# Another order of the same 1418 steps, with 41 changes of ScalarE's table in place of 43

## The chip, the cores and the metric

The kernel runs on one core of one Trainium2 chip. The metric is the device time of one execution in microseconds (us). TensorE (PE) multiplies matrices, VectorE (DVE), ScalarE (ACT) and GpSimd (POOL) work on elements, SyncE (SP) issues most transfers (DMA). Each engine takes its own instructions strictly in order; between engines, semaphores make a step wait for what it reads.

## The reference

A gated linear attention with a complex decay is followed by a gated feed-forward block with a residual. Inputs are q, k, v, a_re and a_im of shape (4, 8, 768, 48): 4 batches, 8 heads, 768 tokens, 48 dimensions a head.

```
a = (a_re, a_im) * min(mag, 0.999) / (mag + 1e-6)          mag = |a_re + i a_im|
for t in range(768):
    S = a[t] * S + k[t] v[t]^T          (complex S of 48 x 48 for each batch and head)
    y[t] = q[t] . Re S
x = y as (3072, 384)
g, val = x @ w_gate, x @ w_val          (384 -> 1536)
out = x + sigmoid(x @ w_res) * ((gelu(g) * val) @ w_out)
```

## The kernel before

The 768 tokens are cut into 6 chunks of 128. A tile is one chunk of one batch, 24 in all. Tiles are taken in 14 units: units 0 and 1 have one tile of chunk 0 each, unit 2 has two, units 3 to 10 have two each (two units to a chunk), unit 11 has two tiles of chunk 5, and units 12 and 13 one each. The body writes out the steps of each unit in three functions.

- `prepare` loads ar, ai, q, k, v (L420), takes ln and exp of a_re (L442, L443), multiplies t by a_im (L445), squares (L448 on ACT or L450), takes another ln (L451) and joins them to the log of the decay (L452, L456). Sums over the tokens of a chunk are matmuls with a triangular mask (L402, or L406 in float32 for units 0 to 2). exp of the sums gives E and Ei (L487, L488); the angle goes through an arctangent (L497), the same kind of sum, a rounding (L524 or L527, L529), an absolute value (L536 or L538) and two sines (L542). q times E and k times Ei (L548) times the sines give the features fQ and fK (L553). Units 0 to 5 transpose the features on PE (L569) and copy them (L377 or L378); units 6 to 13 use DMA transposes issued by SP (L562), four for a unit of two tiles. A row of E and one of the angle are carried to the next chunk by small DMAs that POOL issues (L492, L503, L509).
- `attend` multiplies features (scores, L610), masks them (L615), multiplies with v and the carried state (L626, L628), copies the result x (L377 or L378) and updates the state (L642, L665 to L685).
- `forward` transposes x (L708 on PE, or by DMA), runs the gate and value matmuls (L726), gelu (L736), the product (L737), the residual gate (L748, L751) and the output matmuls (L761), then L765, L768 and the store (L770). A forward of a one-tile unit uses 128 columns a matmul, of a two-tile unit 256.

PE also has 30 warm-up steps of four matmuls (L777). POOL issues the weights' DMAs (L384): w_gate and w_val in two halves of three pieces each, then w_res and w_out.

ACT holds one set of functions at a time: "L" has ln and exp, "T" arctangent and sine, "G" gelu and tanh; squares, copies and roundings run with any. Whenever a step needs another set than the last one, the program puts in a table load (L785 in the trace).

The order of everything is a literal list. `ORDER` has the numbers of all 1418 steps; each engine gets its steps in that order. `PLACE` says on which engine a step runs that could run on several; a step that is not in it takes a default. The core of the loop:

```
for j in order:
    t = self.steps[j]
    for x in t.stores:                       # a buffer is bound when it is first used:
        ...
        x.index = min(range(x.bufs), key=lambda i: row[i])   # the one that came free first in the list
        ...
    if t.act is not None and t.act != table:
        table = t.act
        load(table)
    ins = t.fn()
    if t.port:                               # POOL's steps and some of DVE's: each change of
        if last is not None and last[0] != t.eng:            # engine waits for the step before
            turn(ins, last[1])
        last = (t.eng, ins)
```

So the list also decides which load waits for which buffer (24 of [128, 768] are shared by loads and temporaries), and where DVE and POOL hand over.

Of the kernel before, what the change touches and what calls it, by code (L numbers as in the profile page):

```python
# [47 lines left out]
    53: "POOL", 54: "DVE", 67: "DVE", 77: "DVE", 80: "ACT", 119: "POOL", 120: "POOL", 131: "DVE", 136: "POOL", 137: "POOL",  # L48
    152: "DVE", 155: "ACT", 190: "DVE", 191: "DVE", 210: "DVE", 218: "ACT", 220: "DVE", 224: "DVE", 239: "DVE", 303: "POOL",
    319: "POOL", 324: "DVE", 326: "DVE", 330: "POOL", 336: "DVE", 349: "DVE", 355: "DVE", 359: "DVE", 406: "DVE", 425: "POOL",  # L50
    433: "ACT", 436: "POOL", 439: "DVE", 441: "DVE", 443: "DVE", 447: "POOL", 455: "ACT", 457: "DVE", 458: "ACT", 475: "DVE",
    476: "ACT", 482: "ACT", 523: "DVE", 538: "POOL", 542: "POOL", 550: "ACT", 553: "POOL", 558: "DVE", 560: "DVE", 564: "POOL",
    570: "DVE", 574: "DVE", 593: "ACT", 655: "POOL", 670: "POOL", 673: "DVE", 677: "DVE", 681: "POOL", 690: "ACT", 696: "DVE",
    706: "DVE", 709: "DVE", 710: "DVE", 780: "ACT", 783: "POOL", 788: "DVE", 790: "DVE", 794: "POOL", 803: "ACT", 809: "DVE",
    815: "DVE", 818: "DVE", 825: "ACT", 881: "POOL", 885: "POOL", 899: "DVE", 901: "DVE", 903: "DVE", 906: "POOL", 907: "POOL",
    914: "ACT", 922: "DVE", 931: "DVE", 932: "ACT", 940: "ACT", 979: "DVE", 1006: "ACT", 1009: "POOL", 1016: "DVE",
    1019: "POOL", 1020: "POOL", 1029: "ACT", 1035: "DVE", 1041: "DVE", 1044: "POOL", 1047: "POOL", 1084: "DVE", 1104: "DVE",
    1105: "POOL", 1120: "POOL", 1130: "POOL", 1131: "POOL", 1138: "ACT", 1140: "ACT", 1146: "DVE", 1152: "DVE", 1155: "POOL",
    1213: "DVE", 1227: "POOL", 1232: "DVE", 1234: "DVE", 1237: "POOL", 1238: "POOL", 1245: "DVE", 1312: "POOL", 1318: "POOL",
    1322: "DVE", 1325: "POOL", 1326: "POOL", 1331: "DVE", 1337: "DVE", 1367: "POOL", 1371: "POOL", 1379: "DVE", 1381: "DVE",  # L60
    1390: "ACT", 1396: "DVE", 1416: "DVE",
}
ORDER = [
# [754 lines left out]
```

## Time and profile before

| | |
|---|---|
| median of 3 runs | 241.28 us (240.02 to 242.72) |
| the profiled execution | 243.0 us, span 241.1 us |
| granted TensorE clock | 1.0 throughout |
| ACT table loads | 43, 55.2 us in all |
| HBM read, written | 31.26 MB, 4.72 MB |
| DMA share by queue | 76.1% SP's, 10.3% POOL's |

The span runs from the first to the last instruction of the profile. A row of a timeline has the start, the length, the engine, the source line, the operation, output <- inputs, shapes and the number of instructions that were merged; in brackets stands how long the engine had been idle before it and what ended that.

### The profile page before, as it was taken

To read this page: it belongs to the slowest core of one execution; us is meant where nothing else is said; L and a number is where in the kernel's file an instruction comes from. 1 tells how busy PE (TensorE), PEld (TensorE's weight loads), DVE (VectorE), ACT (ScalarE), POOL (GpSimd) and SP (SyncE) were. 2 spreads that over 40 slices of the span, in tenths; PEclk is the share of its full clock that TensorE was granted. 3 is DMA by queue.
4 is the path that set the end of the run, shared out by engine and by line. 5 is a ranking of instruction groups with operands and counts; after the bars stand their busy time and mean duration, and the time that the engine had idled before them with its cause. 6 is when DMAs were issued, how large, how long until landed. Compare 5 with 4: busy or idle time off the path is not lost. (4 is left out here: it accounts for less than half of the span.)

```text
span 241.1 us, 6430 instructions
## 1 busy us (share of the span) xinstructions
PE 227.3 (94%) x2513; PEld 180.3 (75%) x2513; DVE 203.5 (84%) x361; ACT 203.8 (85%) x326; POOL 135.5 (56%) x152
## 2 busy tenths in 40 slices
PE   6899997999999999999997999998999999998992
PEld 4677896877788778778785777786788687787871
DVE  2477996999998999999998899998999979976162
ACT  5799996999999999999999899999889889942140
POOL 3457975526987446854929727719759564040111
PEclk9999999999999999999999999999999999999999
DMA  7999999999899989999899999899688283680121
GB/s 146 215 212 219 205 197 183 190 202 187 162 214 217 204 172 202 207 211 200 179 202 184 223 195 180 187 218 193 127 120 191 56 154 85 135 123 16 52 98 67
DMA packets 164798, 40.55 MB, mean 168 GB/s; under 512 B 158240, under 2 KB 164768, under 8 KB 164768
## 3 DMA queue, kind: packets, MB, share of 16 engines
q1 hardware_dynamic: 160320, 36.25, 76.1%
q0 software_dynamic: 4448, 3.90, 10.3%
q8 instruction: 19, 0.31, 0.6%
q14 instruction: 11, 0.09, 0.1%
HBM read 31.26 MB, written 4.72 MB: 149 GB/s over the span
## 5 line engine op out<-in xcount | busy, mean ns | idle before, releaser
L726 PE MATMUL pb<-xT,wv 128*128 128x256 bf16 (+1 forms) x504 | 57.0, 257 | 1.7 <-DMA wv<-in_moe_w_val_dram 1.5
L785 ACT ACT_TABLE_LOAD x43 | 55.2, 1283 | 1.5 <-PEq L802 0.7
L761 PE MATMUL pb<-wo,hb 128*128 128x384 bf16 x288 | 54.6, 326 | 0.0
L726 PE MATMUL pb<-xT,wg 128*128 128x256 bf16 (+1 forms) x504 | 53.5, 257 | 0.0
L737 DVE SCALAR_TENSOR_TENSOR hb<-hb,pb 128x512 bf16<-128x512 bf16 x72 | 47.0, 679 | 7.6 <-PE pb L726 7.4
L736 ACT ACTIVATE hb<-pb 128x512 bf16<-128x512 f32 x72 | 39.5, 608 | 14.2 <-PE pb L726 13.8
L726 PEld LDWEIGHTS <-wv 128*128 128x128 bf16 x504 | 42.8, 98 | 8.5 <-DMA wv<-in_moe_w_val_dram 2.2
L726 PEld LDWEIGHTS <-wg 128*128 128x128 bf16 x504 | 42.8, 98 | 5.6 <-DVE xT L378 0.2
L761 PEld LDWEIGHTS <-hb 128*128 128x128 bf16 x288 | 26.3, 97 | 13.7
L615 DVE TENSOR_TENSOR am<-pb,mask 128x512 bf16<-128x512 f32 x48 | 31.2, 683 | 2.8 <-PE pb L610 2.7
L768 POOL TENSOR_TENSOR ot<-ot,x 128x384 f32<-128x384 f32 x19 | 17.2, 909 | 21.1 <-DVE ot L765 17.0
L548 POOL TENSOR_TENSOR Ke<-k,Ei 128x768 bf16<-128x768 f32 (+1 forms) x11 | 18.3, 1662 | 4.9 <-ACT Ei L488 2.2
L445 POOL TENSOR_TENSOR t<-t,ai 128x768 f32<-128x768 f32 (+1 forms) x11 | 16.7, 1516 | 7.2 <-DMA ai<-in_a_im_dram 3.3
L610 PE MATMUL pb<-QT,KT 96*128 96x128 bf16 x192 | 17.2, 219 | 3.7 <-DMA KT<-fK 2.2
L610 PEld LDWEIGHTS <-KT 96*128 96x128 bf16 x192 | 13.1, 97 | 8.3 <-DMA KT<-fK 3.2
L517 POOL TENSOR_TENSOR tl<-t 128x768 f16<-128x768 f32 (+1 forms) x9 | 12.5, 1391 | 11.6 <-DMA t<-fr 5.1
L777 PE MATMUL pb<-tri,ident 128*128 128x256 bf16 x120 | 16.4, 292 | 2.4 <-POOL tri masks.py:66 2.4
L777 PEld LDWEIGHTS <-ident 128*128 128x128 bf16 x120 | 12.4, 105 | 5.6 <-issue 1.8
L765 DVE SCALAR_TENSOR_TENSOR ot<-sg,pb 128x384 f32<-128x384 f32 x24 | 13.0, 547 | 3.5 <-PE pb L761 2.6
L748 PE MATMUL pb<-wr,xT 128*128 128x384 bf16 x72 | 15.5, 326 | 0.0
L452 DVE SCALAR_TENSOR_TENSOR la<-s,la 128x768 f32<-128x768 f32 (+1 forms) x14 | 11.7, 837 | 3.4 <-POOL s L450 2.1
L529 DVE SCALAR_TENSOR_TENSOR fr<-fr,pb 128x384 f32<-128x384 int32 x24 | 12.8, 546 | 1.5 <-ACT fr L524 1.4
(95 smaller groups left out, 446.8 us busy)
## 6 DMA issues: line engine op xcount, KB each, us to landing
ar<-in_a_re_dram SPq DMA_DIRECT2D x24, 192.0 KB, 3.9
ai<-in_a_im_dram SPq DMA_DIRECT2D x24, 192.0 KB, 3.9
k<-in_k_dram SPq DMA_DIRECT2D x24, 192.0 KB, 4.1
q<-in_q_dram SPq DMA_DIRECT2D x24, 192.0 KB, 3.9
vf<-in_v_dram SPq DMA_DIRECT2D x24, 192.0 KB, 3.8
out_dram<-ot SPq DMA_DIRECT2D x24, 192.0 KB, 3.2
wg<-in_moe_w_gate_dram POOLq DMA_DIRECT2D x6, 192.0 KB, 5.6
wv<-in_moe_w_val_dram POOLq DMA_DIRECT2D x6, 192.0 KB, 6.7
```

What stands on the lines that cost most here:

```text
L445: add(e1, "tai", lambda: on[e1].tensor_tensor(out=F("t"), in0=F("t"), in1=flat(T("ai"), n), op=OP.mult), [s["ai"]], [s["t"]], n)
L548: add(e13, "qe", lambda g=g, src=src, mag=mag, e13=e13: on[e13].tensor_tensor(out=T(g + "e")[:, 0:n * H].rearrange("p x u d -> p (x u d)") ...
L610: nc.tensor.matmul(out=view()[:, h, :], lhsT=kT.tile[0:DD, u * H // 2 + h, :], rhs=qT.tile[0:DD, u * H // 2 + h, :], start=True, stop=True)
L615: add("DVE", "am", lambda u=u, am=am, view=view: nc.vector.tensor_tensor(out=am.tile[:, u * H // 2:(u + 1) * H // 2, :], in0=view(), in1=m ...
L726: nc.tensor.matmul(out=o_.at(y, nb, n * 128)[:, u, :], lhsT=w_[:, k_, (nb * m + u) * 128:(nb * m + u + 1) * 128], rhs=xt.tile[:, k_, 0:n]. ...
L736: add("ACT", "gelu", lambda gp=gp, hv=hv: nc.scalar.activation(out=hv(), in_=pv(gp), func=AF.Gelu), gs, [hh], sz, "G")
L737: add("DVE", "h", lambda vp=vp, hv=hv: nc.vector.scalar_tensor_tensor(out=hv(), in0=hv(), scalar=0.5, in1=pv(vp), op0=OP.mult, op1=OP.mult ...
L748: nc.tensor.matmul(out=rp.at(y, DM), lhsT=xt.tile[:, k_, j, :], rhs=wr[:, k_, :], start=(k_ == 0), stop=(k_ == KF - 1))
L761: nc.tensor.matmul(out=op_.at(0, DM), lhsT=hb[k_ // per].tile[:, (u * n + j) * 128:(u * n + j + 1) * 128], rhs=wo[:, k_, :], start=(k_ == ...
L768: add(e8, "otx", lambda s=s, i=i, ot=ot, e8=e8: on[e8].tensor_tensor(out=ot.tile, in0=ot.tile, in1=s["x"].tile[:, i].rearrange("p h d -> p ...
L777: nc.tensor.matmul(out=spare.at(0, 256), lhsT=ident, rhs=tri[:, :].bitcast(BF), start=True, stop=True)
L785: plan.run(ORDER, lambda table: nc.scalar.preload_act_table_set(ACT_SETS[table]), lambda ins, prev: tc.add_manual_dep(ins.ins, prev.ins.na ...
```

## The change

The code is the same; the literals `PLACE` and `ORDER` are new. No step is added or dropped, and no buffer changes in number or size. The start of each list, and the part where unit 7's features are transposed (797 to 800 are its four DMA transposes: QT and KT of its first tile, then of its second; 804, 806 and 810, 812 are the scores of the first and the second tile):

```
-    14, 46, 51, 52, 24, 22, 20, 8, 19, 1, 112, 117, 118, 23, 47, 53, 54, 55, 113, 3, 49, 119, 28, 120, 180, 9, 63, 129, 130,
+    112, 117, 118, 12, 19, 14, 46, 51, 7, 1, 27, 28, 2, 52, 5, 25, 47, 53, 54, 113, 119, 120, 178, 180, 63, 64, 9, 179, 0, 50,
...
-    902, 797, 800, 716, 718, 799, 720, 897, 899, 736, 798, 593, 705, 801, 722, 1099, 887, 876, 890, 891, 1102, 728, 1211, 993,
+    1095, 895, 721, 518, 723, 735, 715, 736, 716, 800, 725, 883, 799, 896, 704, 797, 733, 717, 898, 897, 737, 594, 801, 884,
+    705, 739, 798, 718, 595, 724, 899, 885, 900, 632, 901, 887, 726, 720, 596, 740, 597, 886, 728, 640, 902, 890, 722, 524,
```

What this makes of each engine's own order, read from the two programs (u is the unit, f the group of a forward):

```
POOL, start, before: tai.u0 tai.u1 sq.u1 mrd.u0 w qe.u1 w w mrd.u1 qe.u1 w w w vcast.u1 mrc.u0 vcast.u0 mrc.u1 tai.u3 wr sq.u3 w mrd.u2 w w w carry.u3 w carry.u3 w
POOL, start, after:  qe.u0 qe.u1 w mrd.u0 mrd.u1 w w w qe.u1 w w mrc.u1 tai.u3 wr mrc.u0 w w w w mrd.u2 w carry.u3 carry.u3 w
ACT, start, before:  [L] ln.u0 exp.u0 ln.u1 exp.u1 lnb.u0 [T] atan.u0 atan.u1 [L] ln.u2 lnb.u1 ...
ACT, start, after:   [L] ln.u1 exp.u1 ln.u0 exp.u0 [T] atan.u0 atan.u1 [L] lnb.u0 lnb.u1 ln.u2 ...
DVE, start, before:  sq.u0 la.u0 cap.u0 round.u1 ...
DVE, start, after:   tai.u0 sq.u0 tai.u1 sq.u1 la.u0 cap.u0 la.u1 fr.u0 cap.u1 tai.u2 ...
ACT, end, before:    gelu.f10 x4 [L] pexpE.u12 x.u11 pexpI.u12 [T] sin.u12 x2 x.u11 [L] pexpI.u13 Mc.u10 pexpE.u13 [T] sin.u13 x2 [G] tanh.f10 ...
ACT, end, after:     gelu.f10 x3 [L] pexpI.u13 pexpE.u13 pexpI.u12 x.u11 pexpE.u12 mrc.u10 [T] sin.u12 x2 round.u13 sin.u13 x2 [G] tanh.f10 ...
```

Here w is a weight's DMA, tai the product with a_im, sq the square, lnb the second ln, la and cap the two steps to the decay's log, pexpE and pexpI the exponentials L487 and L488, qe the products L548, mrd and mrc a carried row and its copy, Mc the copy of the matrix made from it.

Steps that are on another engine than before, as the change in count (a two-tile step has 768 columns, a one-tile step 384):

| step | ACT | DVE | POOL |
|---|---|---|---|
| tai, one tile | | 0 to 3 | 4 to 1 |
| square, one tile; two tiles | 1 to 2; 4 to 6 | 1 to 2; 1 to 1 | 2 to 0; 5 to 3 |
| low part of the decay (L460), one tile; two tiles | | 0 to 2; 6 to 3 | 2 to 0; 3 to 6 |
| low part of the angle (L517), one tile; two tiles | | 1 to 0; 1 to 2 | 1 to 2; 8 to 7 |
| absolute value, one tile; two tiles | 1 to 2; 1 to 2 | 3 to 2; 9 to 8 | |
| q or k product (L548), one tile | | 4 to 3 | 4 to 5 |
| v to bfloat16, one tile; two tiles | 1 to 1; 3 to 4 | 1 to 3; 1 to 0 | 2 to 0; 6 to 6 |
| residual sum (L768) | | 5 to 7 | 19 to 17 |
| copies of x, xT, QT and KT, M | 10 to 11, 3 to 4, 5 to 4, 5 to 8 | 14 to 13, 15 to 14, 15 to 16, 6 to 3 | |
| state (Gb copy; Gb; Gf), carried row's copy | 4 to 2; ; ; 4 to 4 | 3 to 5; 1 to 0; 4 to 3; 0 to 2 | 9 to 9; 3 to 4; 8 to 9; 7 to 5 |

More of the change, by code (lines that the diff above doesn't have):

```diff
@@ L47 @@
 PLACE = {
[L48 to L60, printed above, removed]
@@ L61 @@
-    1390: "ACT", 1396: "DVE", 1416: "DVE",
+    54: "DVE", 71: "POOL", 77: "DVE", 78: "DVE", 80: "ACT", 89: "DVE", 110: "DVE", 120: "DVE", 131: "DVE", 133: "DVE",
+    136: "POOL", 137: "POOL", 143: "DVE", 144: "ACT", 146: "ACT", 152: "DVE", 155: "DVE", 190: "DVE", 191: "DVE", 202: "DVE",
+    210: "DVE", 220: "DVE", 222: "ACT", 227: "ACT", 245: "ACT", 307: "POOL", 319: "POOL", 322: "DVE", 326: "DVE", 330: "POOL",
+    336: "DVE", 338: "ACT", 340: "DVE", 349: "DVE", 355: "DVE", 363: "DVE", 421: "POOL", 425: "POOL", 433: "ACT", 436: "POOL",
@@ new lines @@
+    439: "DVE", 441: "DVE", 443: "DVE", 447: "POOL", 457: "DVE", 458: "ACT", 460: "ACT", 466: "DVE", 480: "DVE", 484: "ACT",
+    523: "DVE", 538: "POOL", 542: "POOL", 550: "ACT", 553: "POOL", 558: "DVE", 560: "DVE", 564: "POOL", 570: "DVE", 574: "DVE",
+    583: "DVE", 589: "DVE", 593: "DVE", 634: "DVE", 670: "POOL", 673: "DVE", 677: "DVE", 680: "POOL", 681: "POOL", 690: "ACT",
+    696: "DVE", 702: "DVE", 705: "DVE", 709: "DVE", 710: "ACT", 714: "ACT", 753: "DVE", 772: "POOL", 780: "ACT", 783: "POOL",
@@ new lines @@
+    786: "DVE", 790: "DVE", 794: "POOL", 801: "ACT", 803: "ACT", 809: "DVE", 815: "DVE", 827: "ACT", 880: "DVE", 881: "POOL",
+    885: "POOL", 901: "DVE", 903: "DVE", 906: "POOL", 907: "POOL", 916: "ACT", 922: "DVE", 935: "DVE", 998: "POOL",
+    1006: "DVE", 1016: "DVE", 1019: "POOL", 1020: "POOL", 1027: "ACT", 1029: "ACT", 1041: "DVE", 1044: "POOL", 1047: "POOL",
+    1049: "ACT", 1084: "DVE", 1117: "ACT", 1120: "POOL", 1123: "DVE", 1125: "DVE", 1130: "POOL", 1131: "POOL", 1155: "POOL",
+    1158: "POOL", 1199: "DVE", 1213: "DVE", 1227: "POOL", 1230: "DVE", 1238: "POOL", 1245: "ACT", 1251: "DVE", 1307: "DVE",
@@ L62 @@
+    1318: "POOL", 1331: "DVE", 1377: "POOL", 1381: "DVE", 1384: "POOL", 1385: "POOL", 1390: "DVE", 1416: "DVE",
 }
 ORDER = [
[62 rows of a table removed]
[61 rows of a table added]
 ]
```

118 rows, old and new, of the table ORDER are left out of this document.

## The prediction

> **What bounds the kernel now.** First the page's totals, then the busy times by stage (columns: stretch, its length, then PE, PEld, DVE, ACT, POOL busy with their instruction counts, granted clock, DMA share, GB/s).
>
> ```profile
> span 241.1 us, 6430 instructions
> ...
> PE 227.3 (94%) x2513; PEld 180.3 (75%) x2513; DVE 203.5 (84%) x361; ACT 203.8 (85%) x326; POOL 135.5 (56%) x152
> ```
> ```profile
> 0.00:42.00 42.00, 36.37 (x412) 29.60 (x413) 28.63 (x54) 35.26 (x57) 25.92 (x44) 1.00 1.06 197
> 42.00:108.00 66.00, 66.00 (x743) 52.72 (x741) 63.89 (x113) 65.13 (x98) 42.36 (x42) 1.00 1.01 197
> 108.00:200.00 92.00, 89.20 (x954) 69.78 (x953) 85.24 (x150) 84.95 (x142) 58.99 (x59) 1.00 0.90 172
> 200.00:241.00 41.00, 35.73 (x416) 28.23 (x412) 25.79 (x47) 18.50 (x33) 8.25 (x9) 1.00 0.37 85
> ```
> PE never idles from 42 to 108, while DVE and ACT fill 97 to 99% of that stretch and the transfer engines are full up to there. So the question is how much PE work there is and where PE waits. The timeline of PE gives the price of a matmul from the distance of two starts:
>
> ```profile
> 213.96 1.47 PE L726 MATMUL pb<-xT,wv 128*128 128x256 bf16 x12
> 215.27 0.82 PE L726 MATMUL pb<-xT,wg 128*128 128x256 bf16 x6
> ...
> 222.27 3.41 PE L761 MATMUL pb<-wo,hb 128*128 128x384 bf16 x20
> 225.52 0.83 PE L726 MATMUL pb<-xT,wv 128*128 128x128 bf16 x12
> ...
> 233.82 2.76 PE L761 MATMUL pb<-wo,hb 128*128 128x384 bf16 x16
> ```
> 12 matmuls of 256 columns took 1.31, so 0.109 each; 20 of 384 took 3.25, so 0.1625. The same reading for each shape, times its count (720 of 256 columns 78.5, 288 + 72 of 384 columns 58.5, the rest 84, of which the 120 warm-up matmuls are 13.1), gives 220.9 us of PE work, the same in both lists. What a list decides is the lag: start of a matmul minus the PE work listed ahead of it. The last 16 output matmuls start at 233.82 with 218.25 ahead: lag 15.6. After PE comes a fixed tail (two DVE steps and the last store):
>
> ```profile
> 236.68 0.56 DVE L765 SCALAR_TENSOR_TENSOR ot<-sg,pb 128x384 f32<-128x384 f32 x1 [0.93 <-PE pb L761]
> ...
> 237.34 0.56 DVE L768 TENSOR_TENSOR ot<-ot,x 128x384 f32<-128x384 f32 x1
> ```
> 220.9 + 15.6 + 4.6 = 241.1, the span. So 20 us at most can be touched. Where the lag of 15.6 grows:
>
> ```profile
> 2.38 6.60 PE L777 MATMUL pb<-tri,ident 128*128 128x256 bf16 x44 [2.38 <-POOL tri masks.py:66]
> ...
> 10.07 0.91 PE L406 MATMUL pb<-t,tri 128*128 128x384 f32 x2 [1.09 <-ACT t L497]
> ```
> ```profile
> 27.67 0.83 PE L726 MATMUL pb<-xT,wg 128*128 128x128 bf16 x12
> ...
> 36.49 0.62 PE L610 MATMUL pb<-QT,KT 96*128 96x128 bf16 x8
> 37.21 0.28 PE L726 MATMUL pb<-xT,wv 128*128 128x128 bf16 x2
> 38.34 1.85 PE L726 MATMUL pb<-xT,wv 128*128 128x128 bf16 x30 [0.85 <-DMA wv<-in_moe_w_val_dram]
> 40.89 0.40 PE L726 MATMUL pb<-xT,wv 128*128 128x128 bf16 x4 [0.70 <-DMA wv<-in_moe_w_val_dram]
> ```
> ```profile
> 130.79 0.32 PE L402 MATMUL pb<-ll,mask 128*128 128x384 f16 x1
> 132.62 0.38 PE L610 MATMUL pb<-QT,KT 96*128 96x128 bf16 x4 [1.51 <-DMA QT<-fQ]
> ...
> 168.29 0.62 PE L610 MATMUL pb<-QT,KT 96*128 96x128 bf16 x8 [1.08 <-DMA KT<-fK]
> ...
> 217.60 0.62 PE L610 MATMUL pb<-QT,KT 96*128 96x128 bf16 x8 [0.86 <-DMA KT<-fK]
> ```
> At the first gate matmul (27.67, 21.06 ahead) the lag is 6.6; after the last wait for the second half of the value weights (40.89, with 31.9 ahead) it is 9.0. It hardly grows until 108 (PE busy 66.00 of 66.00), then three waits for transposed features of units 7, 9 and 13 (1.51, 1.08, 0.86) carry most of the rest.
>
> **The change, part by part.** Step kinds and counts per engine are the same but for placement: by the grouped rows of the same shapes ACT takes 3.8 us of work more and two table loads less, net +1.2; DVE -0.1; POOL -6. None is a bound by itself; each counts where PE waits.
>
> *Start.* In the old list the first product t·a_im is POOL's and the squares are split.
>
> ```profile
> 3.73 0.52 ACT L442 ACTIVATE la<-ar 128x384 f32<-128x384 f32 x1 [1.72 <-DMA ar<-in_a_re_dram]
> ...
> 5.63 1.00 POOL L445 TENSOR_TENSOR t<-t,ai 128x384 f32<-128x384 f32 x1 [3.30 <-DMA ai<-in_a_im_dram]
> ...
> 6.66 0.56 DVE L450 TENSOR_TENSOR s<-t 128x384 f32<-128x384 f32 x1 [4.07 <-POOL t L445]
> ...
> 9.08 0.94 ACT L497 ACTIVATE t<-t 128x384 f32<-128x384 f32 x2
> ```
> The new list has products and squares of units 0 and 1 on DVE (0.56 a step, as in the row at 6.66): 5.6 to 7.8 in all. ACT loads the arctangent table right after its fourth step, so both arctangents end near 8.0 against 10.0. Going on with row durations I get the second decay sum near 12.4 and the first scores near 21; in the old run:
>
> ```profile
> 13.72 0.88 PE L406 MATMUL pb<-la,tri 128*128 128x384 f32 x2
> ...
> 23.98 0.61 PE L610 MATMUL pb<-QT,KT 96*128 96x128 bf16 x8
> ```
>  The new list uses up all 30 warm-ups before the first gate matmul, the old one 28, and 22.30 us stand ahead of it instead of 21.06. I get its start at about 27.6, so the lag is 5.3, 1.3 less.
>
> *Second half of the weights.* In the old list POOL issues them between these rows:
>
> ```profile
> 28.48 0.78 POOL L384 DMA_DIRECT2D wv<-in_moe_w_val_dram  x1
> ...
> 35.24 0.57 POOL L384 DMA_DIRECT2D wv<-in_moe_w_val_dram  x1 [1.59 <-DMA mr<-E]
> ```
> The new POOL list has four fewer tensor steps ahead and puts both carries before the last weight only; I get issues from 24.7 to 30. In the old run the last weight was used 5.7 after its issue (35.24 to 40.89); transfers are full (share 1.06), and 24 loads and 13.5 weight units lie ahead in either list, so I take 38.5 for the landing, not 35.7. Needed with 31.28 ahead, that is a lag of 7.3 against 9.0. **Term: -1.7**; ends 0 (the transfers hold it) and -3.
>
> *Transposed units.* SP issues four DMA transposes a unit, one after another:
>
> ```profile
> 125.35 1.42 SPq L562 DMA_TRANSPOSE QT<-fQ  x1
> ...
> 128.31 2.07 SPq L562 DMA_TRANSPOSE QT<-fQ  x1
> 130.43 1.33 SPq L562 DMA_TRANSPOSE KT<-fK  x1
> ...
> 162.75 1.33 SPq L562 DMA_TRANSPOSE KT<-fK  x1
> ```
> For unit 7 the first scores need the third transpose (128.31) in the old list and the second in the new: 1.5 earlier, about what PE waited (1.51). For unit 9 both tiles' scores stood next to each other and waited for the fourth (162.75); now 2.1 us of PE work stand between, more than 1.08. The new list also has no load of inputs right ahead of unit 7's transposes. Together 2.6 removed; late next are the masked scores and products behind them (DVE and ACT are 92% busy there), so I take half. **Term: -1.3**; ends -2.6 and 0.
>
> *Tables at the end.* Both removed loads are here.
>
> ```profile
> 208.43 1.28 ACT L785 ACT_TABLE_LOAD   x1
> 209.72 0.49 ACT L751 ACTIVATE sg<-pb 128x384 f32<-128x384 f32 x1
> ```
> The old list goes exponentials, sines for unit 12, then again exponentials, sines for unit 13; the new one does both units in one pass of each: 2 x 1.28 = 2.6 of ACT less ahead of unit 13's sines, which lets its scores go without the 0.86. **Term: -0.8**; ends -0.9 and 0. The step after the load at 208.43 starts 1.29 later, so a load costs its own 1.28 and no more here. The Trainium skill ("ScalarE: Activation LUTs", What ACT_TABLE_LOAD costs) adds a drain of about 1380 ns to the same load, some 2.66 us for each switch; this trace shows no drain. By that figure the two would be worth 5.3 of ACT time, an estimate, with the same 0.86 of PE wait to remove.
>
> *What gets tighter.* With 160 to 180 us of PE work done, the ACT work that PE needs stands 1.6 to 4 us behind PE's in the new list, 5 to 10 in the old one. ACT idled 7 of 92 us there. **Term: +0.7**; ends 0 and 2.
>
> Sum: -1.7 - 1.3 - 0.8 + 0.7 = -3.1, span 238.0. The profiled execution took 243.0 with its span of 241.1; the median of the runs shown is 241.28, 0.7% below. The difference is applied to the median: 238.2.
>
> **The rivals.** *Features late on DVE (slower).* From unit 8 on the new list puts more DVE work ahead of the features: 1.9 us for unit 8, 2.5 for unit 10, 3.7 for unit 12.
>
> ```profile
> 205.97 0.55 DVE L553 TENSOR_TENSOR fQ<-Qe,CS 128x768 bf16<-128x768 bf16 x1
> ```
> ```profile
> 211.14 0.61 PE L610 MATMUL pb<-QT,KT 96*128 96x128 bf16 x8
> ```
> If DVE's waits do not shrink, unit 12's end at 210.2 instead of 206.5; its scores came 4.6 after that (211.14), and with 197.3 ahead in the new list this is a lag of 17.5, and the last two units' transposes queue behind at 1.4 each, some 18.1 at the end, +2.5 and so 243.8. For: that work must run. Against: DVE idled 6.8 of 92 us there waiting for PE, and a step that is listed earlier fills such a wait. It decides from unit 8 on. The Trainium skill ("SBUF — State Buffer", its part on the shared port pair) speaks for it too: two-input DVE work and POOL's reads shut each other out. No run here shows such a block by itself, since both lists hand over between the two engines in order, 53 times in the old and 56 in the new.
>
> *Transfers set it (no change).* Weights land at 40 whatever POOL does, unit 3's q and k follow as before, and each removed transpose wait is replaced by the masked scores: only -0.8, 240.5. For: share over 1 to 108.
>
> *The tables count for nothing.* ACT is busy 18.5 of the last 41 us, so the named change saves nothing and only the start does: 239.6.
>
> **How the numbers follow.** Forecast 0.45 (own range 235.5 to 238.8), late features 0.21, transfers 0.24, tables 0.10. 1% of this kernel is 2.4 us, about what a measurement can tell from no change: below 238.9 is faster, above 243.7 slower. So faster 0.45 (the forecast), same 0.34 (transfers and tables), slower 0.21 (late features). All gains at their ends give -6.5 (234.8); upward I go past the late features, since a wait on an in-order engine is passed on: 245.5.
>
> **What would show it.** Right: the first gate matmul still near 27.6 and the value weights' wait over by 40; no PE wait over 1 us at unit 7's and 9's scores; lag at the end near 12.5, so the last 16 output matmuls near 231. Wrong: PE idle above 10 us in total, a new wait of PE for transposed features of units 8 to 12, or for masked scores while ACT is full at 165 to 190; a first gate matmul after 28.5.

## The result and the profile after

| | before | after |
|---|---|---|
| median | 241.53 us (17 runs, 240.02 to 245.28) | 240.0 us (17 runs, 237.83 to 244.62) |
| ratio | | 0.9916, 95% interval 0.9888 to 0.9944 |
| profiled execution | 243.0, span 241.1 | 240.16, span 236.9 |
| ACT table loads | 43, 55.2 us | 41, 52.6 us |

Three runs of the new list and one of the old are slow ones (241.5 to 245.3 us), and the ratio compares the means of the others, 239.43 and 241.45; the medians are of all runs. The new list is faster by 0.84% or 2.0 us (1.4 to 2.7). The two profiled spans differ by 4.2, twice that: a span is one execution, and 3.3 us of the profiled one lie outside its span after, 1.9 before. So the ratios below judge, and the spans only show where to look.

First the page's totals of the new list, then its busy times by stage, with the columns of the prediction's windows:

```profile
span 236.9 us, 6443 instructions
...
PE 227.7 (96%) x2513; PEld 181.2 (76%) x2513; DVE 203.2 (86%) x362; ACT 204.9 (87%) x332; POOL 130.6 (55%) x143
```
```profile
0.00:42.00 42.00, 38.18 (x427) 30.77 (x427) 30.63 (x57) 36.80 (x59) 19.91 (x36) 1.00 1.05 194
42.00:108.00 66.00, 65.99 (x726) 52.49 (x726) 64.21 (x114) 64.88 (x98) 47.08 (x43) 1.00 1.01 200
108.00:200.00 92.00, 91.10 (x996) 72.36 (x995) 88.43 (x156) 89.64 (x152) 56.46 (x57) 1.00 0.93 172
```
PE idles 9.2 us in all (before 13.8). From 108 to 200 it does 1.9 more work in the same 92 us, and DVE and ACT do 3.2 and 4.7 more: nobody got faster, all wait less. Now PE's timeline at the places that the prediction named:

```profile
28.54 0.22 PE L725 MATMUL pb<-xT,wg 128*128 128x128 bf16 x1
29.15 3.47 PE L725 MATMUL pb<-xT,wg 128*128 128x128 bf16 x59 [0.39 <-DMA wg<-in_moe_w_gate_dram]
...
39.13 1.40 PE L725 MATMUL pb<-xT,wv 128*128 128x128 bf16 x22 [0.71 <-DMA wv<-in_moe_w_val_dram]
...
130.77 0.61 PE L609 MATMUL pb<-QT,KT 96*128 96x128 bf16 x8
...
167.37 0.61 PE L609 MATMUL pb<-QT,KT 96*128 96x128 bf16 x8 [0.90 <-DMA QT<-fQ]
...
212.80 0.39 PE L609 MATMUL pb<-QT,KT 96*128 96x128 bf16 x4
...
214.17 0.39 PE L609 MATMUL pb<-QT,KT 96*128 96x128 bf16 x4
...
228.37 4.06 PE L760 MATMUL pb<-wo,hb 128*128 128x384 bf16 x24
```
The waits at units 7 and 13 (130.77, 212.80) are gone, unit 9's is 0.90 instead of 1.08 (167.37). The first gate matmul came at 28.54, not at 27.6. The last 24 output matmuls start at 228.37 with 220.9 - 24 x 0.1625 = 217.0 ahead, so the lag at the end is 11.4.

To see where a lag grows, I took it at every step of PE in each profile (start of the step minus the priced work ahead of it). By these prices the old list ends at 15.4. Columns: lag with so many us of PE work done; the last column is the timed ratio to the kernel before.

| list | 40 | 120 | 180 | 220 | ratio (95%) |
|---|---|---|---|---|---|
| before | 9.05 | 10.11 | 14.14 | 15.41 | 1 |
| after | 8.26 | 9.28 | 11.05 | 11.26 | 0.9916 (0.9888 to 0.9944) |
| e1: new to step 350, then old | 8.34 | 9.90 | 13.59 | 14.85 | 1.0035 (0.9998 to 1.0073) |
| e2: old to step 350, then new | 8.39 | 9.65 | 11.35 | 11.55 | 0.9885 (0.9849 to 0.9922) |
| e3: old to 1210, then new | 8.35 | 9.35 | 14.1 | 14.5 | 1.0020 (0.9991 to 1.0049) |
| e4: old, unit 7's transposes | 8.28 | 9.56 | 12.7 | 14.0 | 0.9994 (0.9966 to 1.0023) |
| e5: old, 41 tables | 8.72 | 11.84 | 14.92 | 16.73 | 1.0011 (0.9979 to 1.0042) |
| e6: old to 740, then new | 9.07 | 16.44 | 17.06 | 17.26 | 1.0117 (1.0068 to 1.0167) |
| e7: old to 850, then new | 8.95 | 10.54 | 12.18 | 12.38 | 0.9888 (0.9847 to 0.9929) |
| e8: old to 1090, then new | 8.41 | 9.77 | 14.54 | 14.74 | 1.0010 (0.9982 to 1.0038) |
| e9: old, one store | 8.02 | 9.05 | 12.27 | 12.77 | 0.9953 (0.9929 to 0.9977) |
| e10: old, unit 9's scores | 9.88 | 10.80 | 14.59 | 15.87 | 1.0032 (1.0003 to 1.0061) |
| e11: e4 + e9 + e10 | 7.62 | 10.85 | 13.73 | 14.18 | 0.9989 (0.9956 to 1.0022) |
| e12: new, unit 9's scores | 8.40 | 9.40 | 11.36 | 11.57 | 0.9959 (0.9927 to 0.9992) |

Two stretches tell the lists apart. From 120 to 180 the lag grows by 1.6 to 2.0 where the order there is the new one (after, e2, e7, e12), and by 2.9 to 4.0 where it is the old one (before, e1, e4, e5, e9, e10, e11). From 180 to 220 it grows by 0.2 in the new order, by 1.3 to 1.8 in the old one, and by 0.5 in the old one with a store moved (e9, e11).

### The profile page after: what moved, and what is told of

Read it like the earlier page. It is cut to its first block, busy times and chain, and to the rows that moved or that the text cites. A ratio compares the mean times of both kernels' runs of the same rounds, so it can differ in the third digit from the quotient of the medians.

```text
span 236.9 us, 6443 instructions
## 1 busy us (share of the span) xinstructions
PE 227.7 (96%) x2513; PEld 181.2 (76%) x2513; DVE 203.2 (86%) x362; ACT 204.9 (87%) x332; POOL 130.6 (55%) x143
## 4 chain that ended last, share of the span: by engine, by line
PE 77%; DMA 9%; SPq 4%; DVE 3%; POOL 3%; issue 1%; POOLq 0%; DVEq 0%
PE pb L725 36%; PE pb L760 18%; DMA vf<-in_v_dram 6%; PE pb L401 5%; PE pb L747 5%; PE pb L609 4%; SPq L419 4%; PE pb L568 2%; DMA QT<-fQ 2%; PE pb L625 2%; PE pb L627 2%; PE pb L641 2%; DMA ai<-in_a_im_dram 1%; PE pb L707 1%; POOL Ke L547 1%
## 5 line engine op out<-in xcount | busy, mean ns | idle before, releaser
L725 PE MATMUL pb<-xT,wv 128*128 128x256 bf16 (+1 forms) x504 | 56.3, 257 | 0.7 <-DMA wv<-in_moe_w_val_dram 0.7
L760 PE MATMUL pb<-wo,hb 128*128 128x384 bf16 x288 | 55.3, 325 | 0.0
L784 ACT ACT_TABLE_LOAD x41 | 52.6, 1283 | 1.4 <-PEq L801 0.7
L725 PE MATMUL pb<-xT,wg 128*128 128x256 bf16 (+1 forms) x504 | 52.6, 257 | 0.4 <-DMA wg<-in_moe_w_gate_dram 0.4
L767 POOL TENSOR_TENSOR ot<-ot,x 128x384 f32<-128x384 f32 x17 | 15.4, 911 | 26.9 <-DVE ot L764 15.3
L547 POOL TENSOR_TENSOR Ke<-k,Ei 128x768 bf16<-128x768 f32 (+1 forms) x12 | 19.3, 1612 | 15.7 <-DVE s L449 12.5
L776 PE MATMUL pb<-tri,ident 128*128 128x256 bf16 x120 | 17.0, 302 | 2.4 <-POOL tri masks.py:66 2.4
L516 POOL TENSOR_TENSOR tl<-t 128x768 f16<-128x768 f32 (+1 forms) x9 | 11.9, 1320 | 12.7 <-DVE t L444 5.4
L609 PE MATMUL pb<-QT,KT 96*128 96x128 bf16 x192 | 16.5, 219 | 0.9 <-DMA QT<-fQ 0.9
L459 POOL TENSOR_TENSOR ll<-la 128x768 f16<-128x768 f32 x6 | 8.8, 1463 | 12.6 <-DVE Gf L684 7.6
L444 POOL TENSOR_TENSOR t<-t,ai 128x768 f32<-128x768 f32 (+1 forms) x8 | 13.7, 1713 | 2.3 <-DVE fQ L552 1.7
```

The source lines that it names most:

```text
L444: add(e1, "tai", lambda: on[e1].tensor_tensor(out=F("t"), in0=F("t"), in1=flat(T("ai"), n), op=OP.mult), [s["ai"]], [s["t"]], n)
L547: add(e13, "qe", lambda g=g, src=src, mag=mag, e13=e13: on[e13].tensor_tensor(out=T(g + "e")[:, 0:n * H].rearrange("p x u d -> p (x u d)") ...
L609: nc.tensor.matmul(out=view()[:, h, :], lhsT=kT.tile[0:DD, u * H // 2 + h, :], rhs=qT.tile[0:DD, u * H // 2 + h, :], start=True, stop=True)
L725: nc.tensor.matmul(out=o_.at(y, nb, n * 128)[:, u, :], lhsT=w_[:, k_, (nb * m + u) * 128:(nb * m + u + 1) * 128], rhs=xt.tile[:, k_, 0:n]. ...
L760: nc.tensor.matmul(out=op_.at(0, DM), lhsT=hb[k_ // per].tile[:, (u * n + j) * 128:(u * n + j + 1) * 128], rhs=wo[:, k_, :], start=(k_ == ...
L767: add(e8, "otx", lambda s=s, i=i, ot=ot, e8=e8: on[e8].tensor_tensor(out=ot.tile, in0=ot.tile, in1=s["x"].tile[:, i].rearrange("p h d -> p ...
```

## The experiments

Where a list is made of two, the first so many steps come from one and the rest, without those, stands in the order of the other; each step runs on the engine that its own list gives it.

### e1 and e2: the start alone, and everything but the start

```
e1:  ORDER = new[:350] + (the old list without these)
e2:  ORDER = old[:350] + (the new list without these)
```


> The first 350 steps of the new list (some 52 us of PE work, through the first forwards and unit 3's transposes), then all other steps in the old order; 43 table loads. Theory (each stretch of the list adds its own PE waits and the lag is carried to the end): lag at 60 us of work 8.6 as in the new kernel's profile, not 9.2, then the old waits for units 7, 9 and 13 again, end lag 14.5 to 15: 0.2 to 0.4% faster than before. Rival (the lead of the start is used up, because the old middle part is bound by ACT and DVE): same end lag as before, 15.4, ratio 1.000.

> The first 350 steps of the old list, then all others in the new order; 41 table loads. Theory: lag 9.1 at 60 us of work as before, then growing by 2.7 only (as in the new kernel's profile) to about 12: 1.0 to 1.4% faster in the profile's terms, ratio 0.990 to 0.994 in runs. Rival (the later part of the new list gains only because its start is ahead): end lag above 14.5, ratio 0.998 or more.

The new start alone is not faster (1.0035), and without it nothing is lost (0.9885). PE waits for the second half of the value weights in both; e1's row, then e2's:

```profile
39.36 1.40 PE L727 MATMUL pb<-xT,wv 128*128 128x128 bf16 x22 [0.94 <-DMA wv<-in_moe_w_val_dram]
```
```profile
40.23 0.40 PE L725 MATMUL pb<-xT,wv 128*128 128x128 bf16 x4 [0.82 <-DMA wv<-in_moe_w_val_dram]
```
The eleven profiles with the old start have a lag at 40 of 7.6 to 9.9, mean 8.6; the three with the new one 8.3 to 8.4. The 9.0 that I read before was one draw of this spread.

### e3, e6 and e8: the new order from a later point

```
e3:  ORDER = old[:1210] + (the new list without these)
e6:  ORDER = old[:740]  + (the new list without these)
e8:  ORDER = old[:1090] + (the new list without these)
```


> The first 1210 steps of the old list (178 us of PE work), then the rest in the new order, so that only the last part is new, with one pass of exponentials and one of sines for units 12 and 13: 41 table loads. Theory: PE's wait of 0.86 before unit 13's scores goes, end lag 14.4 to 14.6 instead of 15.4: 0.3 to 0.4% faster. Rival (the two loads lie where ACT is idle anyway and another wait takes the place): ratio 1.000, end lag 15.2 or more.

> The old list for its first 740 steps (108 us of PE work), then the steps that are left in the order of the new list. Theory A (the whole gain lies from unit 7 on): the lag grows by about 2 from there to the end as in the new list (9.3 to 11.3) and not by 5.3 as in the old one; ratio to the kernel before 0.987 to 0.991. Rival B (the order between the steps 350 and 740, where PE never idles, prepares it, by letting DVE and ACT run ahead): the growth is 3.5 or more, ratio 0.995 or above.

> The old list for its first 1090 steps (159 us of PE work, up to behind unit 9's scores), then the steps that are left in the order of the new list. Theory A (the end is a gain of its own): the lag grows by 0.3 to 0.6 behind 160 us of PE work instead of 1.45, ratio to the kernel before 0.995 to 0.997. Rival B (the smaller growth at the end belongs to a list that comes there earlier): growth 1.2 or more, ratio 0.999 to 1.002.

All three made a wait of their own where the lists meet, and so say little on what they were made for. PE's rows there, of e6, e3 and e8:

```profile
125.89 0.66 PE L747 MATMUL pb<-wr,xT 128*128 128x384 bf16 x3 [4.36 <-ACT xT L376]
```
```profile
193.05 0.83 PE L725 MATMUL pb<-xT,wg 128*128 128x256 bf16 x6 [0.71 <-DVE Gf L664]
```
```profile
178.61 1.47 PE L724 MATMUL pb<-xT,wv 128*128 128x256 bf16 x12 [0.47 <-ACT hb L734]
```
In e6 a copy on ACT came 4.4 late, and the lag grew by 6.7 from 100 (9.76) to 120; behind it by only 0.8 to the end (the old list: 5.3). Once PE had waited long, hardly anything else was late. In e3 and e8 unit 13's wait of 0.86 is gone, as in the new list, but the waits around the meeting point took it: 0.96 in all in e3, and 1.10 in e8, where PE had also waited 0.63 for a carried row at 173.48.

### e7: the new order from step 850, behind unit 7's scores

```
ORDER = old[:850] + (the new list without these)
```


> The old list for its first 850 steps (125 us of PE work, unit 7's scores included), then the steps that are left in the order of the new list. Theory A (the waits of unit 7 and of unit 9 are two separate losses, about 1.4 us and 1.1 to 1.4 us): unit 7's wait of 1.3 to 1.7 us stays, the growth behind it is about 2 instead of 3.5 to 4, ratio to the kernel before 0.993 to 0.996. Rival B (what unit 7 waits gives the later units their slack; whichever is late first pays for all): behind a kept wait at unit 7 the rest grows by less than 1, ratio 0.989 to 0.992. Rival C (the order before it is what the rest needs): unit 9's wait stays too, ratio 0.997 or above.

0.9888: the whole gain of the new list, with the old start and the old transposes of unit 7, whose wait is still there:

```profile
132.23 0.38 PE L609 MATMUL pb<-QT,KT 96*128 96x128 bf16 x4 [0.69 <-DMA QT<-fQ]
```
By its ratio this is what Rival B gave, and the lag behind unit 7 grew by 0.9, just under the 1 that it had named. The stretch from 124 to 180 us in four profiles (before, after, e7, e9), columns as above:

```profile
124.00:180.00 56.00, 53.20 (x554) 41.45 (x552) 51.10 (x89) 52.15 (x87) 35.41 (x35) 1.00 0.98 182
```
```profile
124.00:180.00 56.00, 55.10 (x589) 43.84 (x587) 52.89 (x93) 54.63 (x93) 35.12 (x34) 1.00 1.02 183
```
```profile
124.00:180.00 56.00, 55.31 (x584) 43.93 (x582) 53.28 (x92) 54.10 (x93) 34.96 (x34) 1.00 0.95 179
```
```profile
124.00:180.00 56.00, 53.79 (x569) 42.27 (x568) 51.91 (x90) 52.36 (x88) 36.86 (x37) 1.00 1.02 184
```
With the new order PE does 1.9 to 2.1 us more here than in the old list, and DVE and ACT with it; e9 (below), which has the old order in this stretch, stands near the old list.

### e4, e10 and e11: the waits for transposes, taken away in the old list

```
e4:   902, -797, +799, 800, 716, 718, -799, +797, 720, ...
e10:  ... 1038, 1101, -1032, 948, 935, 819, 1039, 1209, -1030, -1033, 962, ..., -1031, 975, +1032, +1030, +1033, +1031, 1123, 1040, ...
e11:  e4, e10 and e9 (below) together
```


> The old list with one change: unit 7's DMA transposes are issued with the second tile's Q and K first (its scores come first), so that the first scores need the second transpose and not the third. Theory: PE's wait of 1.5 at unit 7 falls to 0.3 or less and the 1.2 is kept: end lag 14.2, 0.5% faster. Rival (what is late next takes it: masked scores, or unit 8's transposes, which stood at the edge themselves): the wait at unit 7 goes, but the lag is back at 12.4 after unit 8 and 15.4 at the end, ratio 1.000.

> The old list with one edit: unit 9's second pair of scores and their masks stand behind two more groups of PE's matmuls (1.3 us of work), DVE's order is unchanged. Theory A (the wait of 1.08 is a loss of its own): no wait at these scores, lag growth from 140 to 180 us of PE work 0.5 to 0.8 instead of 1.6, ratio to the kernel before 0.995 to 0.996. Rival B (as with unit 7's transposes alone, the later units take it back): ratio 0.999 to 1.001, with the waits moved to unit 10 to 13 or to masked scores.

> The old list with three edits together: unit 7's third transpose first (as in the run that had it alone), unit 9's second pair of scores 1.3 us of PE work later, unit 13's second transpose ahead of the store. Engine assignments, tables (43), ACT's order and DVE's order stay. Theory A (the waits for transposes are the whole difference between the lists): lag at the end 11.8 to 12.5, ratio to the kernel before 0.989 to 0.992, like the new list. Rival B (what the new list gains comes from steps on other engines and in another DVE order, which give every unit from 8 on its features earlier): waits move on, ratio 0.996 or above.

In e4 unit 7's wait is gone, and units 8, 9 and 13 wait:

```profile
146.30 0.40 PE L610 MATMUL pb<-QT,KT 96*128 96x128 bf16 x4 [0.58 <-DMA KT<-fK]
...
166.87 0.62 PE L610 MATMUL pb<-QT,KT 96*128 96x128 bf16 x8 [1.18 <-DMA KT<-fK]
```
In e10 unit 9's scores (168.43) do not wait. They start when they started before (168.29); the two groups of matmuls that used to cover the steps behind them have been spent, and PE waits 0.60 for the copied result of the same unit and 0.64 for unit 10:

```profile
168.43 0.61 PE L610 MATMUL pb<-QT,KT 96*128 96x128 bf16 x8
...
171.59 0.34 PE L708 MATMUL pb<-ident,x 128*128 128x128 bf16 x3 [0.60 <-DVE x L378]
...
184.10 0.38 PE L610 MATMUL pb<-QT,KT 96*128 96x128 bf16 x4 [0.64 <-DMA QT<-fQ]
```
The 1.08 came back as 1.24, and e10 is no faster than before, rather slower. e11 is not what Theory A asked (0.989 to 0.992): 0.9989, where the product of the three single ratios is 0.9979. So it came out as Rival B said, waits move on and the ratio is above 0.996; that the order of the other engines is the reason is not shown by this run. Here a wait for a transpose in the middle of the kernel shows that something is late, and moving the scores past it makes PE wait elsewhere.

### e5 and e9: unit 13's wait, by the tables and by one store

In the old list, ACT's rows, DVE's rows, one row of POOL and SP's queue around unit 13:

```profile
205.91 1.28 ACT L785 ACT_TABLE_LOAD   x1
207.47 0.53 ACT L542 ACTIVATE CS<-fw 128x384 bf16<-128x384 f32 x1 [0.27 <-DVE fw L538]
```
```profile
207.02 0.36 DVE L538 TENSOR_SCALAR fw<-fr 128x384 int32<-128x384 int32 x1
...
208.69 0.56 DVE L553 TENSOR_TENSOR fK<-Ke,CS 128x768 bf16<-128x768 bf16 x1
```
```profile
212.11 0.92 POOL L768 TENSOR_TENSOR ot<-ot,x 128x384 f32<-128x384 f32 x1
```
```profile
210.80 1.24 SPq L562 DMA_TRANSPOSE QT<-fQ  x1
213.05 0.33 SPq L770 DMA_DIRECT2D out_dram<-ot  x1
213.43 2.19 SPq L562 DMA_TRANSPOSE KT<-fK  x1
```
The table load ended at 207.19, and the first sine waited past it for DVE's absolute value. On SP the store at 213.05 waited for its residual sum on POOL (212.11 + 0.92), and the second transpose, whose feature was done at 209.25 (208.69 + 0.56), stood behind it.

```
e5:  ... 1184, 1170, +1374, +1373, 1324, 1323, ..., 1380, -1374, 1330, 1381, 1140, 1154, -1373, 1383, ...
e9:  ... 1333, 1335, 1199, -1200, 1389, +1200, 1336, ...
```


> The old list with one edit: unit 13's two exponential steps stand ahead of unit 12's sines, so both units' exponentials and then both units' sines share a table, 41 loads instead of 43. Theory A (the loads held unit 13's features, as the term of -0.8 says): PE's wait of 0.86 us at unit 13's scores goes, lag at the end 0.8 lower than in the old list's run (15.4 to 14.6), ratio to the kernel before 0.996 to 0.997. Rival B (unit 13's features hang on the order of DVE's steps between 203 and 211, not on ACT): the wait stays at 0.7 to 1.0 us with ACT 2.6 us shorter, ratio 0.999 to 1.001. Rival C: unit 13's exponentials, now ahead of unit 12's sines on ACT, make unit 12 late by their 2 us, and the lag grows by up to 1: ratio 1.002 to 1.004.

> The old list with one edit: the store of group 10's first half, which waits on SP for a residual sum and holds unit 13's second transpose behind it (210.80, then 213.43 in the old run), stands behind that transpose. The tables stay at 43. Theory A (unit 13's 0.86 us are a transpose blocked at the head of SP's queue): issues 1.4 apart, the wait of PE at unit 13's scores below 0.2, lag at the end 0.8 to 1.0 lower than with the store in front, ratio to the kernel before 0.996 to 0.997. Rival B (the scores go earlier, but the masked scores, gelu and output of the last two groups set the end anyway): the wait is gone and turns up behind it, ratio 0.999 to 1.001.

e5 loads 41 tables and gains nothing (1.0011): the sines wait for DVE that much longer.

```profile
202.71 1.28 ACT L785 ACT_TABLE_LOAD   x1
204.01 0.52 ACT L542 ACTIVATE CS<-fw 128x384 bf16<-128x384 f32 x1
...
209.13 0.52 ACT L542 ACTIVATE CS<-fw 128x384 bf16<-128x384 f32 x1 [3.75 <-DVE fw L538]
```
The two loads were worth 2.6 us of ACT; ACT's idle time here is 3.75 instead of 0.27. PE still waits 0.80 at unit 13's scores. The features came no earlier (the first transpose goes out at 212.22 instead of 210.80, of which 0.8 is this run's larger lag), and the store still stands between the two transposes, so e5 does not show what the tables are worth with that store out of the way:

```profile
212.22 1.24 SPq L562 DMA_TRANSPOSE QT<-fQ  x1
214.46 0.33 SPq L770 DMA_DIRECT2D out_dram<-ot  x1
214.84 2.08 SPq L562 DMA_TRANSPOSE KT<-fK  x1
```
e9 keeps 43 tables and gains 0.47% or 1.1 us (0.6 to 1.7) by one store that stands one place later. SP's queue and PE's scores in e9:

```profile
208.93 1.24 SPq L562 DMA_TRANSPOSE QT<-fQ  x1
210.22 1.34 SPq L562 DMA_TRANSPOSE KT<-fK  x1
211.65 0.56 SPq L770 DMA_DIRECT2D out_dram<-ot  x1
```
```profile
214.05 0.82 PE L726 MATMUL pb<-xT,wv 128*128 128x256 bf16 x6
214.96 0.62 PE L610 MATMUL pb<-QT,KT 96*128 96x128 bf16 x8
```
The transposes are 1.3 apart instead of 2.6, and the scores wait 0.25 at most (214.05 + 6 x 0.109 = 214.71). The new list does the same, with both transposes ahead of that store:

```profile
206.58 1.28 SPq L561 DMA_TRANSPOSE QT<-fQ  x1
207.95 1.28 SPq L561 DMA_TRANSPOSE KT<-fK  x1
211.76 1.15 SPq L769 DMA_DIRECT2D out_dram<-ot  x2
```

### e12: the new list without its last large wait

```
... 1026, 970, 1025, 1033, 1126, -1038, 1115, 1131, -1036, 976, 958, +1038, +1036, +1039, +1037, 1214, 1112, 1215, -1039, 1034, 1207, -1037, ...
```


> The new list with one edit: unit 9's second pair of scores, where PE still waits 0.90 us, and their masks stand behind two more groups of PE's matmuls (1.3 us of work). Theory A (PE is still free to gain there): the wait goes, lag at the end 10.4 instead of 11.3, ratio to the kernel before 0.987 to 0.989 where the new list has 0.9916. Rival B (DVE and ACT, busy 88.4 and 89.6 of the 92 us from 108 to 200 in the new list, set the pace): the wait turns up at a later unit, ratio 0.990 to 0.993. Rival C (masks 0.4 us later make unit 10's features late): slower than the new list, 0.994 or above.

```profile
167.70 0.61 PE L609 MATMUL pb<-QT,KT 96*128 96x128 bf16 x8
...
169.47 0.20 PE L625 MATMUL pb<-v,am 128*128 128x48 bf16 x1 [0.76 <-DVE am L614]
```
The wait of 0.90 for a transpose is gone, and 0.76 for the masks on DVE stands 1.8 us behind it. DVE was not late with them. It had itself been idle, waiting for these scores:

```profile
168.12 1.29 DVE L614 TENSOR_TENSOR am<-pb,mask 128x512 bf16<-128x512 f32 x2 [1.25 <-PE pb L609]
```
In the new list 1.3 us of PE work (four output and six value matmuls, 167.81 to 169.12) stand between these scores and the products, and cover the masks. The edit put that work ahead of the scores, so that nothing covers the masks, as in e10 nothing covered the copied result. The lag at 180 is 11.36, against 11.05 without the edit, and the ratio 0.9959 is no better than the new list's 0.9916 (the intervals overlap). It lies where Rival C put it, but unit 10's scores do not wait; and Rival B, by which DVE and ACT set the pace, is not what this row shows.

None of the lists is surely better than the new one. e2 and e7 have lower ratios (0.9885, 0.9888), with intervals that overlap the new list's.

## Why the prediction was right, and where it was not

The forecast was faster, with 238.2 us; it is faster, with 240.0. That lies inside the range as a whole (234.8 to 245.5), but above the forecast's own part of it (235.5 to 238.8) and between the figures of two rivals, 239.6 and 240.5. The size was off: forecast -3.1, measured -2.0. Relative to before, 0.84% is less than the 1% that the text took as its bound, so by that bound alone the outcome counts as "within 1%", to which the text gave 0.34. Of its signs of being right, PE idle below 10 us (9.2), the value weights by 40 (39.13) and no wait over 1 us at units 7 and 9 came; of its signs of being wrong, a first gate matmul after 28.5 came too (28.54).

- *Start, -1.7: wrong, measured nothing.* e1 bounds it between 0 and +1.8, e2 shows no loss without it. Two steps failed. First, the early end of the arctangents (8.40 against 10.02) did not carry through: PE's first sum in the new list waits for nobody and follows straight behind 40 warm-up matmuls, which took 7.07 us, because 24 of them ran 0.21 apart (16 in the old list's run):

```profile
2.38 7.07 PE L776 MATMUL pb<-tri,ident 128*128 128x256 bf16 x40 [2.38 <-POOL tri masks.py:66]
9.29 0.81 PE L405 MATMUL pb<-t,tri 128*128 128x384 f32 x2
```
Second, the last of the second-half weights was not issued by 30:

```profile
25.94 2.18 POOL L383 DMA_DIRECT2D wv<-in_moe_w_val_dram  x4
28.66 0.56 POOL L383 DMA_DIRECT2D wv<-in_moe_w_val_dram  x1
33.36 0.58 POOL L383 DMA_DIRECT2D wv<-in_moe_w_val_dram  x1 [0.41 <-DMA wv<-in_moe_w_val_dram]
```
It went out at 33.36, behind both carries, and PE got it at 39.13, 5.8 later (5.7 in the old run). Above all, the term was the difference between one trace's 9.0 and a computed 7.3 (38.5 - 31.28 is 7.2), and this lag scatters by 2.3 us between executions of the same start. The end of 0 was in the text ("the transfers hold it"); the value was taken from the wrong end.
- *Transposed units, -1.3: the size about right by luck, the reason not.* Beyond e9's 1.1, the new order from step 850 brings 0.9 us (0.9953 to 0.9916) to 1.6 us (to e7's 0.9888), a difference of ratios whose intervals overlap. But it isn't unit 7's transposes (e4: 0.9994; e7 keeps them old) nor unit 9's scores by themselves (e10: 1.0032). "Late next are the masked scores and products" was the right sentence, and taking half for it was too little: alone, these edits give back everything. What took the gain back where a row shows it was the loss of cover behind the moved scores (e10, e12).
- *Tables at the end, -0.8: the wait went, by another cause.* Unit 13's 0.86 is gone, and taking away its cause is worth 1.1 by e9. The step "which lets its scores go without the 0.86" failed: the row at 207.47 says that the sine waited for DVE, not for the load, and I had counted the loads ahead of the sines without reading what ended the idle time behind them. In the new list, too, unit 13's first sine waits for DVE, and for longer than a load takes:

```profile
203.49 0.53 ACT L541 ACTIVATE CS<-fr 128x384 bf16<-128x384 f32 x1 [1.72 <-DVE fr L528]
```
The named change, 41 tables for 43, is worth nothing in the old list (e5); the new list with 43 was not run. The trace still agrees with a load that costs its own 1.28: the sine at 204.01 starts 1.30 after the load's start, without the drain of about 1380 ns that the Trainium skill ("ScalarE: Activation LUTs", What ACT_TABLE_LOAD costs) adds.
- *ACT tighter, +0.7: not seen.* ACT is busy for 89.64 of 92 us, and the one wait of PE over 0.5 between 100 us and the end is 0.90 for a transpose. Its end of 0 was the right one.
- *Late features (0.21): did not come.* DVE's idle time took the earlier work, as the text said against it (85.24 to 88.43 of 92). e12 is no case of it either: there DVE waited 1.25 for PE, not PE for a busy DVE.
- *Transfers (240.5) and tables (239.6)* are near the measured time, but neither as a mechanism: the first kept only the end, while the units gained as well; the second kept only the start, which gave nothing.

In sum: 0 for the start, -0.9 to -1.6 for the units, -1.1 for the end, 0 for ACT, which is -2.0 to -2.7 against the measured -2.0. The lower end agrees by construction, since it is what is left of the measured ratio; the upper end rests on e7. So the direction came out right by two terms whose causes were not those that the text gave, and the errors at the start (1.7 too much) and on ACT (0.7 too little) partly cancelled. What stays open is which of the steps between 850 and 1210 save the 0.9 to 1.6: the joins inside and behind this stretch made waits of their own (e3, e8), and the moves that I could name there brought nothing alone. The windows show only that PE, DVE and ACT all do about 2 us more work in the same 56.

## What to carry to other kernels

Before an idle time on the path is put down to a costly neighbour (a table load, a weight load), read what ended it, and look in the issuing queue for a waiting transfer ahead of the one that is late: here one store, moved by one place, was worth over half (1.1 of 2.0 us, both with wide intervals) of what a new list of 1418 steps brought. Where three engines are over 90% busy, a wait shows the place where a loss becomes visible, not a loss that can be taken away by itself; count it as nothing until the work behind it is shown to be early, and ask what the matmuls that are moved ahead of it had covered. And a term read from one execution, above all one that hangs on transfers at the start, needs the spread between executions beside it.

## What the runs showed that I had not expected

- At the start the distance of the warm-up matmuls falls from 0.21 to 0.109 us at a different time in each execution: 5.7 us from the start of the span in the old list's profile, 7.7 in the new one's, 5.7 to 8.3 over the fourteen profiles, which is 3.4 to 5.9 after the first matmul. The page's row of the granted clock reads full speed all that time. The Trainium skill ("TensorE: Matmul & The Clock Gate", Part 1: The HAM clock gate) puts the change around 4 us into sustained matmul activity, give or take 0.5. Of the fourteen profiles five lie within that (3.8 to 4.4), one below it (3.4) and eight above (4.6 to 5.9).
- The lag at 40 us of PE work, behind the value weights, scattered between 7.6 and 9.9 over eleven profiles of the same start, as much as the whole gain of the change.
